# DeltaNet and SwiGLU in one kernel: where VectorE's queue holds the inverse steps, behind or ahead of the recurrence

## Chip, cores and metric

The kernel runs on one core of one Trainium2 chip. The metric is the device time of one launch in microseconds. A core has TensorE (PE; its weight loads are shown as PEld), VectorE (DVE), ScalarE (ACT), GpSimd (POOL) and SyncE (SP, which here only starts DMA transfers). Each takes its instructions from a queue of its own, and they wait for each other with semaphores.

## What is computed

```python
# q, k, v: (4, 8, 768, 48) float32; beta: (4, 8, 768)
k_n = k / (np.linalg.norm(k, axis=-1, keepdims=True) + 1e-06)
state = np.zeros((B, H, D, D))
for t in range(S):
    kt, vt, bt = k_n[:, :, t], v[:, :, t], beta[:, :, t, None]
    y[:, :, t] = np.einsum('bhd,bhde->bhe', q[:, :, t], state)
    v_old = np.einsum('bhde,bhd->bhe', state, kt)
    state = state + bt[..., None] * np.einsum('bhd,bhe->bhde', kt, vt - v_old)
x = y.transpose(0, 2, 1, 3).reshape(3072, 384)
g = x @ w_gate                                     # 384 x 1536
out = (g * (1 / (1 + np.exp(-g))) * (x @ w_val)) @ w_out   # 1536 x 384
```

A recurrence over 768 positions (DeltaNet, a linear attention with a corrected update of its state) feeds a feed-forward block with a gate. All is float32.

## The kernel before, in words

**Tiling.** The 768 positions are cut into 12 chunks of 64. A chunk holds 64 positions of all 4 batches, 256 tokens. Inside a chunk the recurrence is written as matrix products: it needs the inverse of a triangular 64 x 64 matrix for each of the 32 pairs of batch and head. Inverses are made for two chunks at once, a *group* g.

**The two strands.** TensorE's main work is the feed-forward block of chunk c. `gate_val(c, f)` (L818) makes the gate and value products of two of the 12 blocks of 128 hidden units, 12 matmuls of 128 x 128 by 128 x 256, lets ScalarE take the Silu (L834), and lets VectorE multiply it with the value product into h (L840). It is called for f = 0, 2, 4, 6, 8, 10. Then the output product follows: in chunks 0 to 2 `output` (L848), 12 matmuls for each half of the tokens; from chunk 3 (`FAST`) `output_fast` (L928). The latter has seven products of six matmuls, in the manner of Strassen, instead of eight. For these, VectorE makes sums of h right after the h of f = 6, 8 and 10 (`sums_of_h`, L920 to L926), differences in L965 and L966, and additions of partial results (recorded in L947, called from L957, L960, L968, L976 and L979). The last product, L978, adds into the bank that L968 reads.

Woven into it is the work for later chunks, in pieces. `point(c + 1)` (L1069) issues one piece at most. It is either one of four stages of the recurrence of chunk c + 1 (`advance`, L708) or one stage of preparation (`prep_step`, L1042). The pieces that matter here:

- `advance`, first stage: VectorE scales v (L379); TensorE makes p_r and p_y from the state (L720, L729); VectorE subtracts p_r from v (L737). Second stage: TensorE's p_u (L741). Third stage: TensorE's p_s and p_y (L772, L760); VectorE adds p_s to the state (L781). Fourth stage: the chunk's result is turned (L805, L808).
- Preparation: `turned` (L388) lets VectorE transpose the next k and q (L400, from qpad to kt and qt), and starts SyncE's loads of the ones after them (L401). One point later, `gram` makes the products p_g of k with k and of q with k on TensorE (L422); VectorE copies them out, the first to a_sb (L445), the second through a mask to p_sb (L437).
- `join`: products that put the halves of a finished inverse together.

**The inverse steps.** `invert(g)` (L619) is a generator. Its start is three transposes of a_sb into mb on VectorE (L455, L458), a power on GpSimd (L633), then small VectorE operations that wait for it (L641 to L475). Then come 31 steps of substitution, each a multiplication (L488) and a dependent addition (L494) on VectorE; at last transposes of the result. `fill(n)` (L1088) takes up to n steps out of this generator. `gate_val` calls fill(2) after the Silu and fill(3) at its end; `output_fast` has fill(2), fill(2) and fill(7).

**The order.** The order of each engine's queue is written by hand: the whole part is recorded under a manual schedule (L1112), so every engine gets its instructions in the order in which the Python code issues them. VectorE is the only engine that does the inverse steps in the chunks in question, apart from GpSimd's power and a memset. The main loop of chunks 2 to 11 stands in L1233 to L1244.

Of the kernel before, what the change touches and what calls it, by code (L numbers as in the profile page):

```python
# [20 lines left out]
def kernel(  # L21
# [51 lines left out]
    def ps_ffn(shape, name):  # L73
        return psum.tile(shape, FP32, name=name, tag="ffn", bufs=4)
# [220 lines left out]
    for b in range(2):  # L295
# [5 lines left out]
            fill=0.0,  # L301
# [21 lines left out]
    def new_n(g):  # L323

        n_t[g] = work.tile([128, 2, HH], FP32, name="n_t")
# [138 lines left out]
    def new_mb():  # L464
        return work.tile([128, R, R], FP32, name="mb", bufs=1)
# [349 lines left out]

    hs = {}

    def gate_val(c, f, fill, within=None):  # L818

        ps = {}  # L820
        for w_sb, name in ((wg_sb, "p_gate"), (wv_sb, "p_val")):
            ps[name] = ps_ffn([128, 2, TOK], name)
            for i in range(2):
                for t in range(KT):
                    nc.tensor.matmul(  # L825
                        ps[name][:, i],
                        w_sb[:, t, (f + i) * 128 : (f + i + 1) * 128],
                        xts[c][:, t],
                        start=(t == 0),
                        stop=(t == KT - 1),  # L830
                    )
            if name == "p_gate":
                sil = ffn_pool.tile([128, 2, TOK], FP32, name="sil", bufs=1)
                nc.scalar.activation(sil, ps[name], ACTF.Silu)  # L834
                fill(2)
                if within is not None:
                    point(within)
        at = len(hs) if c < 2 else (len(hs) - 12) % 8
        hs[c, f] = hp[at].rearrange("p (i n) -> p i n", i=2)
        nc.vector.tensor_tensor(out=hs[c, f], in0=sil, in1=ps["p_val"], op=ALU.mult)  # L840
        if c >= FAST:
            if f >= FT // 2:
                sums_of_h(c, f)
            elif combos:
                combos.pop(0)()
        fill(3)

    def output(c, bp, fill, between=()):  # L848
# [71 lines left out]
    def sums_of_h(c, f):  # L920
        f1 = f - FH
        nc.vector.tensor_tensor(
            out=s_of(1, f1), in0=h_of(c, f1, 1), in1=h_of(c, f, 1), op=ALU.add
        )
        minus(s_of(2, f1), s_of(1, f1), h_of(c, f1, 0))
        minus(h_of(c, f1, 1), h_of(c, f1, 0), h_of(c, f1, 1))  # L926
# [60 lines left out]
    def converts(n):  # L987
        if todo:
            convert(todo[:n])
            del todo[:n]  # L990
# [3 lines left out]
    def step(kind, fn, *args):  # L994
        key = (kind, args or (1,))
        if key not in gens:
            gens[key] = [fn(*args), 0]
        next(gens[key][0], None)
        gens[key][1] += 1

    def steps(kind, *args):
        return gens.get((kind, args), (None, 0))[1]
# [34 lines left out]
    def may_advance(c):  # L1037
        g = c // 2
        due = {0: 1, 1: 2 + 2 * (c % 2)}.get(g, 2)
        return steps("advance", c) > 0 or (c in p_sb and steps("join", g) >= due)  # L1040
# [28 lines left out]
    def point(c):  # L1069

        mine = c < NCH and steps("advance", c) < 4 and may_advance(c)
        if mine and steps("advance", c) > 0:
            step("advance", advance, c)
        elif not prep_step(c - 1) and mine:
            step("advance", advance, c)
# [12 lines left out]
    def fill(n):  # L1088
        if todo:

            filled.append(n)
            converts(2 if len(filled) < 4 else 1)
            if len(filled) == 1:
                converts(1)
        else:
            after_weights()
            fill_some(n)
# [3 lines left out]
    def after_weights():  # L1101
        if not done:
            done.append(1)
            nc.gpsimd.memset(ztp[1], 0.0)
            fills.insert(0, (1, second_inverse[0]))
# [6 lines left out]
    with tc.manual_schedule(  # L1112
        engines={
            mybir.EngineType.PE,
            mybir.EngineType.Activation,
            mybir.EngineType.DVE,
            mybir.EngineType.SP,
            mybir.EngineType.Pool,
        }
    ):  # L1120
        new_n(0)
        for at in range(0, 16, 2):
            load_beta(at)
            load_beta(at + 1, nc.sync)
        first_tiles()
        norms(0)

        nc.vector.memset(places[0][:, 0:1], 0)
        norms(1)
        for n in range(4):  # L1130
            stage(n)
        load_q(0)
        load_k(2)
        load_k(3)
        for n in range(4, 10):
            stage(n)
        load_v(0)
        load_q(1)
        stage(10)
        stage(11)  # L1140
        copy_a, copy_v = nc.scalar.copy, nc.vector.tensor_copy
        turned(0, False)
        turned(1, False, "py")
        p_g = [first_gram(0, "px"), first_gram(1, "py")]
        first_diag(0, 0, p_g[0], copy_a)
        first_diag(0, 1, p_g[0], copy_v)
        copy_a(beta_b, beta_s.rearrange("p (g r) -> p g r", g=NG)[:, :, 0:R])
        first_diag(1, 0, p_g[1], copy_a)
        r_b = first_n()
        first_diag(1, 1, p_g[1], copy_v)  # L1150
        mb = new_mb()
        nc.vector.transpose(
            mb.rearrange("p j i -> p (j i)"), first_of["flat"]
        )
        for n in range(12, 17):
            stage(n)
        load_v(1)
        zb = first_scale(mb, r_b)
        for c in range(2):
            first_below(c, p_g[c])  # L1160

        turned(0, True, "ffn")
        turned(2, False, "px")
        turned(3, False, "py")
        first_q = gram_steps(0, True, "ffn")
        next(first_q)
        gram(2, False, "px", (copy_a, copy_a))
        gram(3, False, "py", (copy_a, copy_a))
        for n, _ in enumerate(substitute(mb, zb)):
            if n == R // 2:  # L1170
                for i in range(4):
                    power_step(i)
        m_1 = turned_m(1, "ffn")
        scale_v_heads(0)
        turned(1, True, "px")
        for _ in late_z(0, zb):
            pass
        mb = new_mb()
        mbs.append(mb)
        first_join = join_late(0, 0, ("px", "py"))  # L1180
        next(first_join)
        converts(2)
        next(first_q)
        next(first_join)
        nc.scalar.copy(mb[:, m_1[0][0]], m_1[0][1])
        step("advance", advance, 0)
        converts(2)
        step("advance", advance, 0)
        nc.scalar.copy(mb[:, m_1[1][0]], m_1[1][1])
        converts(2)  # L1190
        step("advance", advance, 0)
        converts(2)
        step("advance", advance, 0)
        converts(2)
        second_inverse.append(invert(1))
        for _ in range(2):
            next(second_inverse[0])
        second = join_late(0, 1, ("ffn", "py"))
        converts(2)

        def state_and_join():
            step("advance", advance, 0)
            next(second)

        def second_join():
            next(second)
            gens["join", (0,)] = [None, 2]

        first.extend((state_and_join, second_join, lambda: gram(1, True)))


        pairs = [(c, f) for c in range(2) for f in range(0, 8, 2)]
        pairs += [(c, f) for f in range(8, FT, 2) for c in range(2)]
        for c, f in pairs:
            early = c == 0 and f < 8
            if c == 1 and f == 0:
                finish(1)
            elif f > 0:
                point(1 if early else 2)
            need((6, 12, 18, 18, 24, 24)[f // 2])  # L1220
            gate_val(c, f, fill, 1 if early else None)
        need(len(pieces))
        for bp in range(NB):
            point(2)
            output(0, bp, fill, (4, 8))
        output(1, 0, fill, (4, 8))
        hold.clear()
        first_blocks(True)
        first_blocks(False)
        point(2)  # L1230
        output(1, 1, fill, range(2, FT, 2))
        finish(2)
        for c in range(2, NCH):  # L1233
            for f in range(0, FT, 2):
                point(c + 1)
                gate_val(c, f, fill)
            point(c + 1)
            if c >= FAST:
                output_fast(c, fill)
            else:  # L1240
                output(c, 0, fill)
                point(c + 1)
                output(c, 1, fill)
            finish(c + 1)  # L1244
# [30 lines left out]
```

## Time and profile before

| what | before |
|---|---|
| median of 3 runs | 737.07 us (736.52 to 737.8) |
| profiled execution, its own time | 735.33 us |
| its span, first to last instruction | 733.5 us |
| TensorE busy | 696.3 us (95%) |
| VectorE busy | 447.2 us (61%) |
| ScalarE busy | 167.4 us (23%) |
| GpSimd busy | 54.2 us (7%) |
| span up to chunk 2's first gate matmul | 188.2 us, TensorE busy 158.6 |
| from there to the end | 545.3 us, TensorE busy 537.7 |
| inverse steps on VectorE, L488 and L494 | 63.2 and 63.7 us, 186 each |
| mean granted TensorE clock | 0.97; 1.00 in every chunk from 2 on |

All times of instructions are counted from the start of the span. In a timeline each line gives the start, the length, the engine, the source line, the operation, what is written and read with its shape, and how many instructions were merged (x12). A bracket at its end says how long the engine had been idle and what ended that. In lists of waits the columns are the total, how often, and the longest. Each float32 matmul has two records. Ends of matmuls are modelled, so records that follow each other can overlap a little.

### The profile page before, as it was taken

What the parts mean: (1) busy time and instruction counts of PE and PEld (TensorE: products, weight loads), DVE (VectorE), ACT (ScalarE), POOL (GpSimd) and SP (SyncE); (2) the same over time, 40 slices, a digit from 0 to 9 for tenths busy, and PEclk for the clock granted to TensorE, in tenths of its full rate; (3) what the DMA queues carried; (4) which work ended last, traced back from release to release, by engine and by line L of the source; (5) the groups of instructions that cost most, each with busy time, mean ns of one, the idle gap of its engine ahead of it and who ended that gap; (6) DMA issues with size and microseconds to landing.
All of it is one profiled execution on the core that took longest, in us unless ns stands there. A gap on an engine that the chain in (4) does not pass through costs nothing.

```text
span 733.5 us, 22491 instructions
## 1 busy us (share of the span) xinstructions
PE 696.3 (95%) x10132; PEld 603.8 (82%) x10132; DVE 447.2 (61%) x904; ACT 167.4 (23%) x323; POOL 54.2 (7%) x46
## 2 busy tenths in 40 slices
PE   4757999999999999999999999999999999999997
PEld 3646888856787789988989988988988988989987
DVE  5995756797597252769853678853678853313122
ACT  3567664202401102021012021012021012021010
POOL 7003000203000000040000040000040000000000
PEclk9557999999999999999999999999999999999999
DMA  6786453310231112421202331202211100100000
GB/s 147 174 242 174 98 142 109 40 26 19 51 46 24 23 23 45 61 51 25 42 4 45 49 64 20 46 3 45 44 25 19 26 3 3 23 2 0 23 1 21
DMA packets 130736, 37.19 MB, mean 51 GB/s; under 512 B 122864, under 2 KB 125936, under 8 KB 130640
## 3 DMA queue, kind: packets, MB, share of 16 engines
q1 hardware_dynamic: 127184, 34.01, 22.7%
q10 hardware_dynamic: 3072, 1.57, 1.0%
q8 instruction: 79, 1.29, 0.8%
q0 software_dynamic: 384, 0.17, 0.1%
q14 instruction: 17, 0.14, 0.1%
HBM read 31.01 MB, written 4.72 MB: 49 GB/s over the span
## 4 chain that ended last, share of the span: by engine, by line
PE 84%; DVE 9%; ACT 4%; issue 2%; POOL 1%; DMA 1%; ACTq 0%; SPq 0%; DVEq 0%
PE p_gate L825 24%; PE p_val L825 23%; PE p_o L937 17%; PE p_o L854 6%; PE p_g L422 3%; DVE tmp L488 3%; DVE zb L494 3%; PE p_u L741 2%; PE p_r L720 2%; PE p_s L772 1%; PE p_y L760 1%; PE p_y L729 1%; POOL n_t L343 1%; PE p_f L805 1%; ACT last_h L250 1%
## 5 line engine op out<-in xcount | busy, mean ns | idle before, releaser
L825 PE MATMUL p_gate<-x_ffn,wg_sb 128*128 128x256 f32 x864 | 204.5, 387 | 1.3 <-ACT x_ffn L808 1.3
L825 PE MATMUL p_val<-x_ffn,wv_sb 128*128 128x256 f32 x864 | 198.5, 379 | 0.0
L825 PEld LDWEIGHTS p_val<-x_ffn,wv_sb 128*128 128x128 f32 x864 | 163.8, 190 | 22.3
L825 PEld LDWEIGHTS p_gate<-x_ffn,wg_sb 128*128 128x128 f32 x864 | 161.2, 191 | 24.1 <-ACT x_ffn L808 1.8
L840 DVE TENSOR_TENSOR h_f<-sil,p_val 128x512 f32<-128x512 f32 x71 | 48.5, 684 | 162.9 <-PE p_val L825 162.7
L834 ACT ACTIVATE sil<-p_gate 128x512 f32<-128x512 f32 x72 | 43.0, 597 | 292.2 <-PE p_gate L825 268.5
L937 PE MATMUL p_o<-wo_sb,h_f 128*128 128x192 f32 x432 | 75.6, 328 | 0.1
L937 PEld LDWEIGHTS p_o<-wo_sb,h_f 128*128 128x128 f32 x432 | 70.3, 190 | 1.2 <-DVE o_sb L947 0.7
L488 DVE TENSOR_TENSOR tmp<-zb,mb 128x31 f32<-128x31 f32 (+15 forms) x186 | 63.2, 340 | 12.0 <-PE p_j L608 6.7
L494 DVE TENSOR_TENSOR zb<-zb,tmp 128x31 f32<-128x31 f32 (+15 forms) x186 | 63.7, 342 | 6.4
L633 POOL TENSOR_TENSOR n_b<-mb,half 128x32 f32<-128x32 f32 x5 | 30.5, 6091 | 408.2 <-DVE mb L458 369.7
L947 DVE TENSOR_TENSOR o_sb<-o_sb,p_o 128x192 f32<-128x192 f32 x45 | 15.7, 349 | 53.7 <-PE p_o L937 36.5
L854 PE MATMUL p_o<-wo_sb,h_f 128*128 128x384 f32 x136 | 45.7, 490 | 0.0
L854 PEld LDWEIGHTS p_o<-wo_sb,h_f 128*128 128x128 f32 x136 | 25.3, 190 | 16.5
L937 PE MATMUL p_o<-last_k,h_f 128*128 128x192 f32 x180 | 32.2, 326 | 0.0
L937 PEld LDWEIGHTS p_o<-last_k,h_f 128*128 128x128 f32 x180 | 29.7, 190 | 0.0
L895 DVE TENSOR_TENSOR h_f<-h_f,h_f 128x256 f32<-128x256 f32 x54 | 22.4, 423 | 8.0 <-PE p_o L937 7.1
L937 PE MATMUL p_o<-last_h,h_f 128*128 128x192 f32 x144 | 26.3, 326 | 0.0
L937 PEld LDWEIGHTS p_o<-last_h,h_f 128*128 128x128 f32 x144 | 23.9, 190 | 0.0
L741 PEld LDWEIGHTS p_u<-vin,zt 64*64 64x64 f32 x768 | 13.7, 141 | 5.8 <-issue 3.2
L458 DVE STREAM_TRANSPOSE mb<-a_sb 32x1024 f32<-32x1024 f32 x8 | 17.1, 2139 | 0.2
L741 PE MATMUL p_u<-vin,zt 64*64 64x48 f32 x768 | 15.7, 228 | 1.3 <-ACT zt L616 1.1
(180 smaller groups left out, 673.4 us busy)
## 6 DMA issues: line engine op xcount, KB each, us to landing
vin<-in_v_dram SPq DMA_DIRECT2D x96, 48.0 KB
kn<-in_k_dram SPq DMA_DIRECT2D x40, 96.0 KB
out_dram<-o_sb SPq DMA_DIRECT2D x36, 96.0 KB
zt<-in_moe_w_out_dram SPq DMA_DIRECT2D x6, 384.0 KB
staged<-in_moe_w_out_dram SPq DMA_DIRECT2D x6, 384.0 KB
qpad<-in_q_dram SPq DMA_DIRECT2D x36, 64.0 KB
wo_sb<-in_moe_w_gate_dram SPq DMA_DIRECT2D x4, 512.0 KB
wo_sb<-in_moe_w_val_dram SPq DMA_DIRECT2D x4, 512.0 KB
```

What stands on the lines that cost most here:

```text
L422: nc.tensor.matmul(p_v[par][half_of(b if of_q else b ^ par), bp, j], kt[c][half_of(par), bp, j, b], xt[half_of(par), bp, j, b],)
L458: nc.vector.transpose(out(rows, 0), in_(rows, 0))
L488: nc.vector.tensor_tensor(out=t_v, in0=zb[:, 0 : j + 1, j : j + 1].to_broadcast([128, j + 1, m]), in1=mb[:, j : j + 1, j + 1 : R].to_broad ...
L494: nc.vector.tensor_tensor(out=zb[:, 0 : j + 1, j + 1 : R], in0=zb[:, 0 : j + 1, j + 1 : R], in1=t_v, op=ALU.add,)
L633: nc.gpsimd.tensor_tensor(out=n, in0=mb.rearrange("p j i -> p (j i)")[:, 0 : R * R : R + 1], in1=half, op=ALU.pow,)
L741: nc.tensor.matmul(p_u[half_of(b), par, bp, j], zt[half_of(b ^ par), par, bp, j], r[half_of(b ^ par), par, bp, j], start=first, stop=True, ...
L825: nc.tensor.matmul(ps[name][:, i], w_sb[:, t, (f + i) * 128 : (f + i + 1) * 128], xts[c][:, t], start=(t == 0), stop=(t == KT - 1),)
L834: nc.scalar.activation(sil, ps[name], ACTF.Silu)
L840: nc.vector.tensor_tensor(out=hs[c, f], in0=sil, in1=ps["p_val"], op=ALU.mult)
L854: nc.tensor.matmul(p_o, hs[c, f - f % 2][:, f % 2, bp * 128 : (bp + 1) * 128], wo_sb[:, f], start=(f == 0), stop=(f == FT - 1),)
L895: nc.vector.tensor_tensor(out=out, in0=a, in1=b, op=ALU.subtract)
L937: nc.tensor.matmul(p[x, part], a(f - f % 2)[:, f % 2], b(f), start=not begun and f == 0, stop=f == FH - 1, skip_group_check=True,)
```

## The change

From chunk 2 on, `point` is called inside `gate_val`, between the h and the three inverse steps of fill(3), and no longer after them. The number of points stays the same: one before the first gate_val of a chunk, and one for each of the six.

```diff
-    def gate_val(c, f, fill, within=None):
+    def gate_val(c, f, fill, within=None, behind=None):
@@
             elif combos:
                 combos.pop(0)()
+        if behind is not None:
+            point(behind)
         fill(3)
@@
         for c in range(2, NCH):
+            point(c + 1)
             for f in range(0, FT, 2):
-                point(c + 1)
-                gate_val(c, f, fill)
-            point(c + 1)
+                gate_val(c, f, fill, behind=c + 1)
             if c >= FAST:
```

Lines of the kernel after are two higher between L846 and the main loop, and one higher after it.

## The prediction

> **What bounds the kernel now.** I read the busy time by stage first, cut where a chunk's first gate matmul starts. Chunk 4 is 303.20:358.66, chunk 5 358.66:414.60. Columns: window, length, busy time of PE, PEld, DVE, ACT, POOL, granted clock, DMA share, GB/s.
>
> ```profile
> 303.20:358.66 55.46, 54.08 (x684) 48.48 (x684) 45.47 (x94) 7.24 (x13) 7.34 (x3) 1.00 0.31 48
> 358.66:414.60 55.94, 55.94 (x939) 50.26 (x938) 29.05 (x53) 8.84 (x15) 0.00 (x0) 1.00 0.15 27
> ```
>
> TensorE fills chunk 5 and lacks 1.4 us in chunk 4, where VectorE has 45.5 us of work against 29.1. Chunks 6 and 8 look like 4, chunks 3, 7 and 9 like 5. From chunk 2 on I therefore ask only where TensorE waits for VectorE. The waits of the PE over the whole run name it:
>
> ```profile
> PE p_g L422 <- DVE kt L400: 2.2, 2, 1.3
> PE p_g L422 <- DVE qt L400: 1.0, 1, 1.0
> ```
>
> Three waits, 1.29 us in chunk 4, 0.94 in chunk 6, 1.04 in chunk 8: **3.3 us in all**. Each is the Gram product p_g waiting for VectorE's transpose of k and q (chunk 8: q alone). The timeline of chunk 4, VectorE's rows, then TensorE's:
>
> ```profile
> 340.10 0.42 DVE L494 TENSOR_TENSOR zb<-zb,tmp 128x256 f32<-128x256 f32 x1
> 340.83 1.25 DVE L400 STREAM_TRANSPOSE kt<-qpad 128x1024 f32<-128x1024 f32 x1 [0.30 <-issue]
> 342.00 1.20 DVE L400 STREAM_TRANSPOSE qt<-qpad 128x1024 f32<-128x1024 f32 x1
> ...
> 342.13 1.16 PE L422 MATMUL p_g<-kt 64*64 64x64 f32 x64 [1.29 <-DVE kt L400]
> ```
>
> The transposes stand behind three inverse steps that began at 337.82; TensorE was free at 340.84. This looks like 3.3 us to win. But the end of the same stage must be read too, VectorE's rows, then TensorE's:
>
> ```profile
> 355.03 1.09 DVE L895 TENSOR_TENSOR h_f<-h_f,h_f 128x256 f32<-128x256 f32 x3
> 356.04 0.76 DVE L947 TENSOR_TENSOR o_sb<-o_sb,p_o 128x192 f32<-128x192 f32 x2
> ...
> 355.59 0.81 PE L937 MATMUL p_o<-last_h,h_f 128*128 128x192 f32 x4
> 356.44 1.92 PEld L937 LDWEIGHTS p_o<-wo_sb,h_f 128*128 128x128 f32 x12 [0.33 <-DVE o_sb L947]
> ```
>
> The chunk's last product (L978) adds into a bank that VectorE reads just ahead, in L968 (recorded in L947, the first of the two at 356.04). Its weights load at 356.44, when that read ends, and it starts with them; the product before it ended at 356.40. TensorE and VectorE arrive there **together**. And VectorE runs without a gap from h of f=6 (329.92) to that read, but for the 0.30 us above. So in chunk 4 VectorE's 26.1 us of work are a limit of their own, as long as TensorE's own work plus its wait. Chunk 6 repeats this: product ended 467.43, next start 467.48 with 0.34 us of PEld idle put down to the same add. Chunk 8 doesn't, having one transpose and two copies fewer:
>
> ```profile
> 575.81 0.35 DVE L947 TENSOR_TENSOR o_sb<-o_sb,p_o 128x192 f32<-128x192 f32 x1
> ...
> 577.20 2.11 PE L937 MATMUL p_o<-wo_sb,h_f 128*128 128x192 f32 x12
> ```
>
> There the read ends at 576.16, 1.04 us ahead of TensorE.
>
> One row more. VectorE's run in chunk 4 begins after 2.06 us of idle time (2.06 in chunk 6, 2.00 in chunk 8), and its earlier work starts from a GpSimd result:
>
> ```profile
> 309.59 2.15 DVE L458 STREAM_TRANSPOSE mb<-a_sb 32x1024 f32<-32x1024 f32 x1
> 311.77 0.96 DVE L379 TENSOR_TENSOR vin<-vin,n_t 128x768 f32<-128x768 f32 x1
> 311.82 6.21 POOL L633 TENSOR_TENSOR n_b<-mb,half 128x32 f32<-128x32 f32 x1 [126.75 <-DVE mb L458]
> 312.83 0.95 DVE L737 TENSOR_TENSOR vin<-vin,p_r 128x768 f32<-128x768 f32 x1
> ...
> 318.06 0.90 DVE L641 TENSOR_SCALAR n_b<-n_b 128x32 f32<-128x32 f32 x1 [1.29 <-POOL n_b L633]
> ...
> 329.92 0.69 DVE L840 TENSOR_TENSOR h_f<-sil,p_val 128x512 f32<-128x512 f32 x1 [2.06 <-PE p_val L825]
> ```
>
> **What the Trainium skill says.** "PSUM — Partial Sum Buffer", section "Engine vs sequencer instructions": VectorE's queue is strictly first in, first out, while TensorE may load weights early but keeps its matmuls in order. The trace agrees: the transposes, whose data were loaded by 330, did not start before the steps ahead of them, and p_g held up all products behind it. "Perfetto Trace Analysis", section "Optimizing Scalar/DVE Operations": the write-acknowledge half of an operation overlaps with the next one. Agrees, for independent ones: h follows a step that lasts 0.42 after 0.34 us, a step that needs the one before after 0.45. That is the only price of changing the order itself. Same page, section "Tensor Engine Instruction (MATMUL, LD_WEIGHTS)": the ends of matmuls are modelled; so I use TensorE's starts. "SBUF — State Buffer", section "SBUF: two separate sides": a VectorE operation with two SBUF inputs and a GpSimd one that reads SBUF exclude each other. L379 and L633 start 0.05 us apart, and L379 lasts 0.96 as elsewhere; no wait is seen. The change sets them apart, so I price nothing.
>
> **The change, part by part.** The built order of both kernels: the instructions are the same on every engine, and TensorE, ScalarE, GpSimd and SyncE have the same order. Only VectorE's changes: five places in chunk 2, four in each of chunks 4, 6 and 8. The other chunks have no inverse steps behind an h. Nothing is added or removed; with VectorE as the only mover, all cost is in who waits.
>
> *Chunk 2.* TensorE waits for VectorE nowhere there. The largest new stall is the state addition after h of f=10: TensorE's p_s ends near 228.71, VectorE is there at 228.35, so 0.36 us, and the transposes behind it end at 237.7 instead of 237.33. Their reader (p_j L684) runs at 245.91. **0.**
>
> *Chunks 4, 6, 8, f=0.* Scaling v (L379) and the subtraction (L737) move ahead of the third transpose of mb. p_r ended at 309.66, the subtraction would start at 310.65: no stall. The transpose starts 1.06 + 0.87 = 1.93 us later (spacing L379 to L737, then L737 to an independent follower: 219.89 to 220.76), so does GpSimd's power, and so do L641 and all behind it: 318.06 becomes 319.99. The steps run on to the last at 327.51, and moving the state addition (next part) makes two steps dependent neighbours, about +0.1. VectorE is ready for h of f=6 at 329.8 against 329.92 (chunk 6: 441.20 against 441.31; chunk 8: 552.31 against 552.35). The idle 2.06 us cover it, with 0.04 to 0.11 to spare: **0**, and every further 0.1 us would be paid. The gain, r ready earlier, is hidden: p_u (315.90) never waited.
>
> *f=4.* The state addition goes ahead of three steps. p_s ended at 323.5, h is done after 325: no stall. Its reader is in the next chunk. **0.**
>
> *f=8.* The transposes move ahead of three steps and start at 337.8 instead of 340.83. kt and qt are done at 339.1 and 340.3, before TensorE asks at 340.84; the wait goes: 1.29, 0.94, 1.04, and in chunks 4 and 6 some 0.06 of gap between the two Grams. SyncE's loads into qpad, issued when a transpose is done, go some 3 us earlier; their reader is a chunk later. **-1.35, -1.0, -1.04** at this place.
>
> *f=10.* Copies of p_g (L445, L437) go ahead of three steps. p_g is done near 343, they start at 346.6: no stall. h of f=10 keeps its time, as the same work stands ahead of it; s2 (L925) for the second product is ready at 346.4, and TensorE, 1.35 earlier, asks at 346.45. **0.**
>
> *The stage's end.* Here the gain meets VectorE's limit. Its chain from h of f=6 to L968 has the same operations. Two steps become dependent neighbours: 0.46 for 0.37, so +0.1 with small change. The 0.30 us before kt may stay (it is "issue") or go (-0.36).
> - Chunk 4: TensorE could be there at 355.1, VectorE lets it go at 356.44 + 0.1. **+0.1** (-0.26 if the gap goes).
> - Chunk 6: 467.48 + 0.1. **+0.1.**
> - Chunk 8: VectorE at 576.16 + 0.1 + 0.06 of handover = 576.32; TensorE's own time 577.20 - 1.04 = 576.16. It starts at 576.32, 0.88 early, and a product that waited takes 2.05 us (356.44 to 358.49) instead of 1.95 (577.20 to 579.15). **-0.78.**
>
> Sum: 0.1 + 0.1 - 0.78 = **-0.6 us**. What is late next is VectorE itself. Against the profiled execution, span 733.50 and 735.33 with what lies around it, that is 734.7; the same off the median of the runs, 737.07, gives **736.5**.
>
> **Rivals.**
> - *The waits are simply gone.* 3.3 us off: 733.8, or 735.0 if one of chunks 4 and 6 keeps its gain. For it: the waits by name, and TensorE idle nowhere else. Against it: the 0.04 us between 356.40 and 356.44; VectorE would need to save 1.3 us in its chain, where I find at most 0.36.
> - *Slower: GpSimd's power comes too late.* The delay of L633 outgrows the idle 2.06 us, for instance as the subtraction is held longer than p_r's end or the power takes longer. Each us beyond the cover goes through VectorE's gapless chain to the last product of chunks 4 and 6 in full, and eats chunk 8's gain. At 0.8 us beyond: +0.9 +0.9 +0.0 = +1.8, 738.9. It leaves the band of no change from about 0.7 us on. For it: a margin of only 0.04 to 0.11. Against it: 6.21 us for the power in the last four of its five cases in the trace, and p_r done 1 us before it is asked for.
> - *The order doesn't reach the chip.* Excluded by the built order. What remains is that chunk 8 is held too, by 0.2 us more on VectorE per stage: no change, 737.1.
>
> **How the numbers follow.** Against this kernel's spread a measurement tells about 0.2%, 1.5 us, from no change. VectorE's limit as worked out: 0.60. No change at all: 0.07. Waits gone wholly or for the larger part: 0.20. Slower by the power: 0.13. So faster 0.20, same 0.67, slower 0.13. The range goes from 734.6, between the two readings of the first rival, to 738.2, the smaller half of the second; the likeliest case's own bounds, -0.36 for the gap and +0.2 per stage, lie inside.
>
> **What would show it.** Right: p_g no longer waits for kt or qt; a new wait of the last p_o for o_sb, about 1.3 in chunk 4, 1.0 in 6, 0.2 in 8; L641 about 1.9 us later with an idle time before h of f=6 near 0.1. Wrong: the last product of chunk 4 starting more than 0.5 us earlier, counted from the chunk's first gate matmul (53.2 us there); or that h starting late with VectorE busy ahead of it.

## The result and the profile after

| | before | after |
|---|---|---|
| median of 6 runs | 736.74 us (735.87 to 737.80) | 735.59 us (733.86 to 736.42) |
| ratio to before | | 0.9979, 95% interval 0.9964 to 0.9994 |
| profiled execution, and its span | 735.33, 733.5 us | 735.90, 734.0 us |

The changed kernel is 0.2% faster: 1.15 us, with an interval from 0.4 to 2.7. The profiled execution of it is 0.6 us *longer* than that of before. So the two traces cannot be compared by their spans. The part ahead of chunk 2, where no instruction was moved, took 188.22 us before and 189.93 after, and from 189.2 to 190.2 in the traces of the kernels below that leave it alone. From chunk 2 on, though, every chunk without a moved instruction (3, 5, 7, 9, 10 and 11) has the same length within 0.02 us in all ten traces. I therefore compare chunk by chunk, from the start of its first gate matmul in TensorE's timeline to that of the next chunk. All experiments, described further down, are in the same table (us):

| kernel | chunk 2 | 4 | 6 | 8 | chunk 2 to the end |
|---|---|---|---|---|---|
| before | 58.91 | 55.36 | 55.02 | 53.59 | 545.24 |
| after | 58.69 | 55.12 | 55.10 | 52.78 | 544.07 |
| turn_only | 58.89 | 55.09 | 55.08 | 52.77 | 544.20 |
| rest_only | 58.89 | 55.35 | 55.00 | 53.58 | 545.18 |
| relief_before | 58.89 | 55.05 | 54.70 | 53.57 | 544.57 |
| relief_after | 58.68 | 53.89 | 53.89 | 53.00 | 541.83 |
| late_power_before | 60.58 | 55.37 | 55.03 | 53.57 | 546.93 |
| late_power_after | 61.44 | 56.39 | 56.38 | 54.08 | 550.68 |
| scale_alone | 58.89 | 55.36 | 55.01 | 53.58 | 545.21 |
| all_copies_scalar | 58.69 | 53.90 | 53.90 | 52.78 | 541.65 |

The change gives -0.22, -0.24, +0.08 and -0.81 us in the four chunks that it touches, and -1.17 from chunk 2 to the end, next to the 1.15 of the medians.

The waits of TensorE over the whole run, cut to those on VectorE's chain (total, how often, longest). The line numbers after are two higher:

```profile
PE p_o L939 <- DVE o_sb L949: 2.0, 4, 0.6
```

The waits of p_g for kt and qt are gone from the list. In their place p_o waits for o_sb, which it did not do before, twice in chunk 4 and twice in chunk 6. Chunk 4 in the timeline, first the end of its gate part (VectorE, then TensorE), where the transposes now stand ahead of the steps:

```profile
338.99 0.42 DVE L897 TENSOR_TENSOR h_f<-h_f 128x256 f32<-128x256 f32 x1
339.32 1.24 DVE L400 STREAM_TRANSPOSE kt<-qpad 128x1024 f32<-128x1024 f32 x1
...
340.49 1.20 DVE L400 STREAM_TRANSPOSE qt<-qpad 128x1024 f32<-128x1024 f32 x1
341.61 0.38 DVE L488 TENSOR_TENSOR tmp<-zb,mb 128x252 f32<-128x252 f32 x1
...
342.25 1.16 PE L422 MATMUL p_g<-kt 64*64 64x64 f32 x64
...
343.24 1.11 PE L422 MATMUL p_g<-qt,kt 64*64 64x64 f32 x64
344.28 2.22 PE L939 MATMUL p_o<-wo_sb,h_f 128*128 128x192 f32 x12
```

The same two products before:

```profile
343.34 1.16 PE L422 MATMUL p_g<-qt,kt 64*64 64x64 f32 x64
344.44 2.22 PE L937 MATMUL p_o<-wo_sb,h_f 128*128 128x192 f32 x12
```

kt is done 1.7 us before p_g reads it, and the 0.30 us ahead of it are gone. Counted from the chunk's start, p_g begins 37.6 us in (342.25 - 304.62); before it was 39.0 (342.13 - 303.13). Its second half, with q, follows after 0.99 us, before after 1.21. So the first product p_o begins 39.66 us in, where it was 41.31: TensorE is 1.65 us ahead, which is more than the named wait of 1.29. Then the end of the same chunk:

```profile
354.60 0.35 DVE L949 TENSOR_TENSOR o_sb<-o_sb,p_o 128x192 f32<-128x192 f32 x1
...
355.00 1.57 PE L939 MATMUL p_o<-last_k,h_f 128*128 128x192 f32 x8 [0.56 <-DVE o_sb L949]
...
357.29 0.61 DVE L949 TENSOR_TENSOR o_sb<-o_sb,p_o 128x192 f32<-128x192 f32 x2
...
357.69 2.22 PE L939 MATMUL p_o<-wo_sb,h_f 128*128 128x192 f32 x12 [0.47 <-DVE o_sb L949]
```

TensorE stands still twice, 0.56 and 0.47 us, each time until an addition on VectorE has read the bank that it wants to add into. From the first p_o to the last product it now takes 13.41 us, where it took 12.00. The last product begins 53.07 us into the chunk; before it was 53.31. Of 1.65 us, 0.24 are left.

### The profile page after: what moved, and what is told of

It reads as the page before. It is cut to its first block, busy times and chain, and to the rows that moved or that the text cites. A ratio compares the mean times of both kernels' runs of the same rounds, so it can differ in the third digit from the quotient of the medians.

```text
span 734.0 us, 22491 instructions
## 1 busy us (share of the span) xinstructions
PE 699.3 (95%) x10132; PEld 605.3 (82%) x10132; DVE 447.8 (61%) x904; ACT 167.4 (23%) x323; POOL 52.0 (7%) x46
## 3 DMA queue, kind: packets, MB, share of 16 engines
q8 instruction: 79, 1.29, 0.7%
## 4 chain that ended last, share of the span: by engine, by line
PE 77%; DVE 11%; SPq 4%; ACT 3%; issue 2%; DMA 2%; POOL 1%; DVEq 0%; ACTq 0%
PE p_gate L825 25%; PE p_val L825 24%; PE p_o L939 14%; DVE tmp L488 3%; DVE zb L494 3%; PE p_o L856 2%; PE p_g L422 2%; PE p_r L720 1%; PE p_u L741 1%; PE p_s L772 1%; PE p_y L760 1%; PE p_y L729 1%; SPq L119 1%; DMA zt<-in_moe_w_gate_dram 1%; SPq L232 1%
## 5 line engine op out<-in xcount | busy, mean ns | idle before, releaser
L633 POOL TENSOR_TENSOR n_b<-mb,half 128x32 f32<-128x32 f32 x5 | 28.2, 5632 | 412.1 <-DVE mb L458 372.7
L939 PE MATMUL p_o<-last_h,h_f 128*128 128x192 f32 x144 | 26.3, 326 | 0.0
```

The source lines that it names most:

```text
L633: nc.gpsimd.tensor_tensor(out=n, in0=mb.rearrange("p j i -> p (j i)")[:, 0 : R * R : R + 1], in1=half, op=ALU.pow,)
L939: nc.tensor.matmul(p[x, part], a(f - f % 2)[:, f % 2], b(f), start=not begun and f == 0, stop=f == FH - 1, skip_group_check=True,)
```

## Experiments

**The transposes alone.** Which of the moved pieces does the work? `moved` picks the calls of `point` that go ahead of the steps:

```diff
-        if behind is not None:
+        moved = (c, f) in ((2, 2), (4, 8), (6, 8), (8, 8))
+        if behind is not None and moved:
             point(behind)
         fill(3)
+        if behind is not None and not moved:
+            point(behind)
```

> Only the transposes of k and q (L400) are moved ahead of the three inverse steps, after h of f=2 in chunk 2 and of f=8 in chunks 4, 6 and 8; every other piece stays where it was before. Counted from a chunk's first gate matmul to the next chunk's. Theory A (the transposes are all of the gain, and VectorE's chain from h of f=6 to the addition ahead of the last product takes it back in chunks 4 and 6): as the changed kernel, chunk 2 -0.2, chunk 4 -0.2, chunk 6 +0.1, chunk 8 -0.8, sum -1.1 us; no wait of p_g for kt or qt; two waits of p_o for o_sb near 0.5 us in each of chunks 4 and 6; GpSimd's power 6.2 us. Theory B (the loss in chunks 4 and 6 comes from the other moved pieces, the later power above all): the full gain of the waits, chunk 4 -1.3, chunk 6 -1.0, chunk 8 -1.0, sum -3.5 us.

The ratio to before is 0.9989, interval 0.9982 to 0.9997. Chunks 4, 6 and 8 are those of the changed kernel within 0.03 us, with four waits of p_o for o_sb, 2.0 us in all, and the power takes 6.21. Theory B falls: with the power where it was, the gain is lost all the same. Chunk 2 was a miss: -0.02, not -0.2. There the transposes do bring p_g's second half forward by 0.22 us (from 20.12 to 19.90 us into the chunk for the gate matmul behind it), but p_y then starts 1.14 us after p_r, where it was 0.97, and p_u 32.88 us in, as before (32.89). Here the mask's copy out of p_g (L437) and the subtraction (L737) still have three steps ahead of them; the copy ends 26.3 us into the chunk, just before p_y starts at 26.42. So chunk 2 needs more than the transposes. Which of the other pieces it needs was not tried.

**All but the transposes.** The same with `not in`.

> The reverse: all pieces are moved as in the changed kernel except the transposes of k and q, which stay behind the three steps. Theory A: nothing changes in any chunk (0 within 0.1 us each); p_g waits 1.3, 0.9 and 1.0 us for kt and qt as before; the power begins about 1.9 us later and takes 5.4 us, and VectorE is idle some 0.8 us ahead of h of f=6. Theory B: slower, 1 us in each of chunks 4 and 6.

The ratio is 1.0002, interval 0.9994 to 1.0011; the touched chunks differ by at most 0.02 us. The waits of p_g stand as before:

```profile
PE p_g L422 <- DVE kt L400: 2.2, 2, 1.3
PE p_g L422 <- DVE qt L400: 1.0, 1, 1.0
```

In chunk 4, VectorE's L641 comes after 2.44 us of idle time instead of 1.29, and h of f=6 after 0.80 instead of 2.06. That is all the other pieces do from chunk 4 on: they use up cover.

**Two copies less on VectorE, in both kernels.** If two limits stand side by side, taking from one alone must bring little, and from both much.

```diff
-            copies = nc.scalar.copy if k_c < 6 else nc.vector.tensor_copy
+            copies = nc.scalar.copy if k_c < 6 or k_c in (8, 10) else nc.vector.tensor_copy
```

> The kernel before, with the two copies of p_g into a_sb (0.60 us each to the next start) moved from VectorE to ScalarE for k of chunks 8 and 10, that is in the f=10 part of chunks 4 and 6. VectorE's chain gets 1.2 us shorter there, and nothing else is changed. Theory A: two limits of equal length stand side by side before, and TensorE's own one, with its wait for kt, is untouched: -0.1 us in each of chunks 4 and 6, -0.2 in all. Theory C (VectorE's load there is the only limit): -1.1 us in each, -2.2 in all.

The ratio is 0.9991, interval 0.9984 to 0.9998. Chunks 4 and 6 change by -0.31 and -0.32 us: under a third of theory C's sum, three times theory A's. p_g still waits 1.28 us for kt, and no wait is named behind it:

```profile
345.85 2.22 PE L937 MATMUL p_o<-wo_sb,h_f 128*128 128x192 f32 x12
...
357.01 0.81 PE L937 MATMUL p_o<-last_h,h_f 128*128 128x192 f32 x4
357.66 2.11 PE L937 MATMUL p_o<-wo_sb,h_f 128*128 128x192 f32 x12
```

This is the shortest way from the first p_o to the last product in any of the traces of chunk 4: 11.81 us (345.85 to 357.66), where the kernel before took 12.00 (344.44 to 356.44). Chunk 8 of the kernel before, where VectorE is 1.04 us early, takes 11.80 too (565.40 to 577.20), so I take it as TensorE's own. VectorE had then already held TensorE 0.19 us before the change, hidden by the modelled end of the product ahead; and the next chunk starts 1.95 us after the last product here, 2.05 before.

> The changed kernel with the same two copies on ScalarE. Theory A: both limits are shorter now, and the gain of the waits is paid out: chunk 4 -1.2 against before (54.3 us), chunk 6 -1.0 (54.1), no more than 0.2 us of waits of p_o for o_sb in each; with chunk 2 -0.2 and chunk 8 -0.8 the sum is -3.2 us, so 733.5 where before has 736.7. Theory D (the last product is held by something else than VectorE's chain, the additions' bank or the store): as the changed kernel, -1.1 us.

The ratio is 0.9943, interval 0.9931 to 0.9955; the median 732.59 us. Chunk 4 changes by -1.47 and chunk 6 by -1.13. The same edit is worth 0.31 us where the transposes wait behind the steps and 1.23 (55.12 - 53.89) where they don't. Theory D falls. The end of chunk 4, VectorE, then TensorE:

```profile
355.30 0.71 DVE L949 TENSOR_TENSOR o_sb<-o_sb,p_o 128x192 f32<-128x192 f32 x2
...
354.81 0.81 PE L939 MATMUL p_o<-last_h,h_f 128*128 128x192 f32 x4
355.70 2.22 PE L939 MATMUL p_o<-wo_sb,h_f 128*128 128x192 f32 x12
```

No wait is named in chunks 4 and 6 any more. VectorE still comes last, though: its read of the bank ends at 355.65, and the last product starts at 355.70. That is 0.89 us after the start of the records ahead of it, where relief_before has 0.65; from the first p_o to it TensorE takes 12.18 us (343.52 to 355.70), 0.37 more than the 11.81. The sum is -3.41 us for an expected -3.2. Chunk 8, not part of this edit, lost 0.22 of its gain, and the one wait of p_o for o_sb that is left, 0.3 us, stands there: an addition began 0.53 us after the step ahead of it, against 0.32 in the changed kernel. What held it stays open.

**A later power.** My rival for "slower" was that GpSimd's power grows too late.

```diff
+        zb = None
+        if g > 1:
+            zb = work.tile([128, R, R], FP32, name="zb", bufs=1)
+            for _ in range(2):
+                nc.gpsimd.tensor_copy(zb, mb)
         n = work.tile([128, R], FP32, name="n_b", bufs=1)
```

(The tile zb is then handed to `scale_m`, which makes its own otherwise.)

> The kernel before, with two extra copies of mb (128x1024) on GpSimd ahead of the power in each of the three later inverses, so that the power and all of VectorE's steps behind it come later by the time d of the two copies. The trace has no such copy; the memset of the same size takes 0.95 us, so d is 1.9 us or more. Theory A (VectorE's idle time ahead of h of f=6 covers a late power, and what goes beyond is paid one for one by the last product of the chunk): the cover is 2.06, 2.06 and 2.00 us, with 1.0 more in chunk 8. With d = 1.9: 0 in all chunks. With d = 3.8: +1.7 in chunks 4 and 6, +0.8 in chunk 8. Theory E (GpSimd's power is off the path in any case): 0 for every d.

The copies took 2.86 us and the power 5.44, so d was 2.86 + 5.44 - 6.21 = 2.09, just the cover. Chunks 4, 6 and 8 change by +0.01, +0.01 and -0.02 us. The run as a whole is 0.47% slower (0.35% to 0.59%), and here the expectation forgot something: g > 1 holds for the inverse that is begun ahead of chunk 2 too. Just ahead of chunk 2, TensorE's p_j now waits 2.6 us for VectorE's state addition, which stands behind the late power, where it waited 0.5; chunk 2 begins at 192.64 us. Chunk 2 itself is 1.67 us longer, but not by a wait: its first gate product took 4.38 us instead of 2.69, with a granted TensorE clock of 0.61 in that stretch instead of 1.00. Why the clock was lower there was not tested.

> The same two copies in the changed kernel, where the power already begins 1.9 us later, but takes 0.8 less, and VectorE has 0.78 us of cover left and TensorE waits for it at the end of the stage. Theory A: d - 0.78 in each of chunks 4, 6 and 8, that is +1.1 each (+3.4 in all against the changed kernel) with d = 1.9, +3.0 each with d = 3.8. Theory E: 0.

Here d was 2.14, and d - 0.78 = 1.36. Measured against the changed kernel: +1.27, +1.28 and +1.30 us. Chunk 2 is 2.75 us longer, most of it again in its first gate product (5.28 us, granted clock 0.50). TensorE's waits from chunk 3 on:

```profile
PE p_o L945 <- DVE h_f L903: 3.3, 3, 1.2
PE p_o L945 <- DVE o_sb L955: 2.0, 4, 0.6
```

The waits for o_sb are the old ones. New are three waits of p_o for the sums of h, at the start of output_fast instead of its end. The mechanism of the rival holds, and Theory E falls; its delay does not come about in the changed kernel.

**Why the power got shorter.** L379 alone goes ahead of the third transpose, and L737 stays.

```diff
+        if (c, f) in ((4, 0), (6, 0), (8, 0)):
+            scale_v(c + 1)
+            scaled.add(c + 1)
         fill(3)
```

(`advance` then leaves out its own call of scale_v for the chunks in the set `scaled`.)

> The kernel before, with the scaling of v alone (L379) moved ahead of the third transpose of mb in chunks 4, 6 and 8; the subtraction stays behind it, and so beside GpSimd's power. Theory L (the power takes 6.21 us where L379, with both inputs in SBUF, runs beside it, and the two exclude each other): 5.44 us for the power. Theory M (the subtraction from PSUM, or anything else beside it, stretches it): 6.2 us. TensorE: 0 in all chunks in either case.

VectorE and GpSimd in chunk 4:

```profile
310.89 0.93 DVE L379 TENSOR_TENSOR vin<-vin,n_t 128x768 f32<-128x768 f32 x1
311.85 2.14 DVE L458 STREAM_TRANSPOSE mb<-a_sb 32x1024 f32<-32x1024 f32 x1
...
314.02 0.95 DVE L739 TENSOR_TENSOR vin<-vin,p_r 128x768 f32<-128x768 f32 x1
314.07 5.44 POOL L633 TENSOR_TENSOR n_b<-mb,half 128x32 f32<-128x32 f32 x1 [127.59 <-DVE mb L458]
```

The power takes 5.44 us beside the subtraction, which reads PSUM. Where L379, with both inputs in SBUF, starts just ahead of it, it takes 6.21 (before, turn_only, relief_before). The reader of the power tells the same: L641 starts 5.47 us after the start of the power here, and 6.24 before. This is what theory L expected. TensorE's chunks don't move: -0.00 to -0.01. This kernel was run once.

**All the copies on ScalarE.** Is more to be had on this way?

> The changed kernel with all copies of p_g into a_sb on ScalarE, for k of chunks 6 to 11, to see what is left to win. Theory A: as with the two in chunks 4 and 6 alone, 53.9 us in each of these, since the other copies lie where VectorE has time to spare; 0 to -0.3 us more, in chunk 2. Rival: ScalarE's Silu or its copies of v queue up behind the new copies and TensorE waits for them, +0.5 us or more in the chunks that begin with a copy (4, 6, 8).

The ratio is 0.9953, interval 0.9936 to 0.9970; the median 733.20. Chunks 2 to 6 are as in relief_after, and chunk 8 has its gain back; it is 541.65 us from chunk 2 to the end, the least of all, by 0.18. In time the two can't be told apart. Apart from chunk 8, moving the other copies gains nothing. Both beat the kernel before in time. Against the changed kernel both are over 2 us shorter from chunk 2 to the end; in time this is clear for relief_after, whose slowest run (733.06) lies below the changed kernel's fastest (733.86), while the runs of all_copies_scalar overlap with it.

## Why the prediction was right, by its steps

- *Three waits of p_g, 3.3 us, go.* Right: none is left in the trace, and turn_only and rest_only show that it is the transposes alone. But the gain was sized too small. I forecast 1.35, 1.0 and 1.04 us; TensorE reached the first p_o 1.65, 1.30 and 1.12 us earlier. In chunks 4 and 6 some 0.2 us of this is q's half of p_g, which had been held behind k's without a named wait. At the end of the stage it made no difference, since VectorE decided there.
- *VectorE's chain takes the gain back in chunks 4 and 6.* Right, and this was the step that decided. Chunk 6 +0.08 for +0.1, chunk 8 -0.81 for -0.78. Chunk 4 -0.24, the other end of its bound: the 0.30 us of "issue" ahead of kt went, and with them 0.36 of the sum. What I had for it was above all the coincidence of 356.40 and 356.44, and that was in part a modelled end: by relief_before, TensorE could have started 0.19 us earlier. The pair of relief runs shows the two limits without it.
- *The new wait.* I named one wait of the last product, 1.3 us in chunk 4. There are two, 0.56 and 0.47, since the product ahead of it (L970) adds into a bank that VectorE reads late as well (L960); I had not carried the chain to that one. The named waits are 1.03 us together; the way from the first p_o to the last product grew by 1.41 (12.00 to 13.41), so the rest is hidden in modelled ends.
- *Chunk 2: 0.* Wrong by 0.22 us. I took "no wait in the list" for "no wait". q's p_g started 1.15 us after k's, against 0.98 after the change. By turn_only, where it follows after 0.98, it had been held by qt, with the end of the one before drawn over the gap; the 0.22 us then also need other moved pieces. I had quoted that ends are modelled, and used it for two places only.
- *f=0: the power 1.93 us later, covered by 0.04 to 0.11.* The mis-sized term was the power. It got 0.77 us shorter, so L641 came 1.15 us later (16.08 us into chunk 4 against 14.93), and 0.78 us of cover are left. I had priced L379 and L633 apart at nothing because "no wait is seen"; the wait was inside the 6.21.
- *f=10: s2 just in time.* Nearly: a weight load waited 0.18 us for it in chunk 4; no cost remained at the end. TensorE asked 1.65 us earlier, not 1.35.
- *The sum.* -0.6 forecast, -1.17 by chunks, -1.15 by medians. The 0.6 between are 0.36 of the gap ahead of kt and 0.22 of chunk 2. Both errors went the same way, and the range of 734.6 to 738.2 held no change at all too, so the time alone says little for the mechanism. The waits and the chunks do.
- *The rivals.* "Simply gone" falls with the waits of p_o. "Slower by the power" is right as a mechanism, at 1.3 us for 1.36, and absent here. "Doesn't reach the chip" was excluded by the order.

## What to carry to other kernels

A stall of the busiest engine is worth only what the next engine's chain leaves: follow the *releaser* from the stall to the end of its stage, and look for the place where both meet again. If they arrive there together, shorten both or expect little; in chunk 4 each alone gave 0.31 and 0.24 us, and both together 1.47. A wait that isn't named can still be there, since the ends of matmuls are modelled: compare the distance of two starts with that of the same pair in another kernel, as the 0.89 and 0.65 us above. And when two traces differ by less than their start-up does, compare them stage by stage: these stages repeat within 0.02 us, while medians of whole runs needed an interval of 2 us.

## What the runs showed of the hardware

A GpSimd instruction that reads SBUF got longer when a VectorE one with two SBUF inputs started just ahead of it: the power 6.21 us for 5.44, and two copies of 128x1024 2.86 us for 2.14, while the VectorE instruction kept its 0.96. The extra 0.77 and 0.72 us are somewhat less than the 0.9 us for which the two overlapped; why isn't shown. The subtraction, with one input in PSUM, did not do that. This agrees with what the Trainium skill says in "SBUF — State Buffer", section "SBUF: two separate sides": the one that starts first has the shared ports for its whole length. I had quoted it and looked for the wait on the wrong engine and outside the instruction. In this profile the extra time stands inside the GpSimd instruction, with no gap ahead of it.
